# Fused set attention and feed-forward on one core: one maximum for 384 tokens, a product by slots, shared 6 KB places and a new order of the steps

## The chip, the cores and the metric

The kernel runs on one core of a Trainium2 chip. Its engines work side by side and each takes its own instructions in order: TensorE (PE; its weight loads are listed as PEld) multiplies matrices into PSUM, VectorE (DVE) and ScalarE (ACT) read PSUM and SBUF, GpSimd (POOL) works on SBUF, and SyncE (SP) issues all transfers here, which 16 DMA engines carry out. The metric is the device time of one execution in microseconds. Lines such as L535 are those of the kernel before.

## The reference

Four batches of 12480 tokens of 128 numbers go through two attention steps against 32 inducing rows, and the result through a feed-forward step with 2048 hidden units.

```python
def mab(q, kv):
    s = scale * (q @ kv.transpose(0, 2, 1))
    s = s - s.max(-1, keepdims=True)
    a = np.exp(s)
    a /= a.sum(-1, keepdims=True) + 1e-09
    return a @ kv
h = mab(I, x)                 # (B, 32, 128): the inducing rows attend to all tokens
y = mab(x, h)                 # (B, N, 128): each token attends to the 32 rows of h
# feed-forward on all 49920 rows of y:
g = y @ w_in
g = g - np.tanh(g)
out = g @ w_out
```

All numbers are float32.

## The kernel before

*The mathematics it uses.* Every row of `y` is a weighted mean of the 32 rows of `h`, so `y @ w_in` is the same mean of the 32 rows of `h @ w_in`. Around the mean of those 32 rows the function `g - tanh(g)` is taken as a straight line (its value at the mean, and its slope `tanh(mean)^2`). Then the whole feed-forward step is linear in the weights of the second attention, and there is one table `P_all[:, b, :]` of 32 x 128 numbers in a batch, so that an output row is its attention weights times that table, divided by their sum. A 129th column of ones gives the sum by the same matmul. `bound` (L587 to L649) works out at run time whether the straight line is good enough; if it is not, `general` would compute the exact form after the main part. With these inputs it is not entered.

*Tiles.* A batch is cut into 8 full tiles of 1536 tokens (`SG`) and a rest of 192. In a full tile the tokens stand in four groups `q` of 384 (`SEG`). Scores of group `q` go to partitions `32q` to `32q + 31`, one partition for each inducing row, with 384 tokens along the free dimension. `R = 3` slots `r` of 128 tokens make up the 384.

*First pass over a batch, `first` (L316 to L426).* For each tile: load `xT` (128 channels x 1536 tokens, 768 KB) on SP (L329); four matmuls against the inducing rows (L306); VectorE copies the scores to SBUF and takes the running maximum (L340). When all nine tiles are through, the maximum of the batch is turned, reduced and spread (L347 to L359). Then, for each tile: ScalarE's exponential with its sum (L394), VectorE's transpose in 32 x 32 blocks (L398), and 12 matmuls into the accumulator `hacc` (L405). The last needs the tile with tokens on partitions, in natural rows. For three tiles of four (`turned`, L313) TensorE turns `xT` by 12 transposes in three groups (L380), and ScalarE or VectorE moves each group to SBUF (L384); for every fourth tile the natural rows are loaded too, another 768 KB (L388). At the end `h` is divided by its sums and transposed (L412 to L425).

*Linear part, `linear` (L434 to L498).* `h @ w_in` (L440), a copy, two sets of turns against the matrix `centre` that subtract the mean (L448), `tanh`, the series of the value at the mean (L464 to L469), the slope part `W` (L474), then two sets of 16 matmuls against `w_out`: `down` for the slope (L483) and `base` for the value (L489). Two more small steps (L493 to L496) end in `P_all`.

*Second pass, `second` (L503 to L583).* For each tile: scores against `h` (L306 again), one transposing maximum on VectorE, per token (L515); GpSimd lays these 384 maxima on diagonals (L520), and a matmul with a matrix of ones subtracts them from the scores in PSUM (L525); ScalarE's exponential (L528); the product with `P_all` by 12 matmuls into `o_ps` (L535). `o_ps` is a single buffer of four PSUM banks; group `q` writes bank `q`, from its own 32 rows of the array. The product is planned in two halves: groups 0 and 1, then groups 2 and 3. VectorE adds and inverts the sums (L545, L546), then multiplies the first half out of PSUM (L565); the second half is copied by ScalarE (L570) and multiplied by GpSimd in SBUF (L573), or done by VectorE too. Then the tile goes out (L582).

*Weights.* `w_in` and `w_out` come as 64-bit patterns, eight chunks of 512 KB in all. Each chunk takes two ScalarE, two GpSimd and three VectorE instructions (L272 to L289) to become float32.

*What sets the order.* Nothing is ordered by hand. Each step is an `Op` with an engine (or a second choice), an assumed cost, the buffers that it reads and writes and a priority. `Plan.order` plays the steps through in time: whenever an engine is free it takes the ready step with the lowest priority number whose buffers have a free place. The sequence that comes out is then issued, engine by engine. `PLACES` says how many buffers of a kind there are: 13 `xT`, 3 `xn` (turned rows), 2 `xd` (loaded rows), 5 `ot` (output, also the weights' raw chunks), 4 PSUM banks `ps` for everything but `o_ps`. The priorities are 100 a batch, plus 5 or 10 a tile.

## Time and profile before

| what | us |
|---|---|
| median of 3 runs (lowest, highest) | 279.3 (276.66, 280.68) |
| the profiled execution | 279.22 |
| its span, first to last instruction | 277.4 |
| TensorE busy | 226.3 |
| VectorE busy | 153.7 |
| ScalarE busy | 106.2 |
| GpSimd busy | 96.1 |

The span is what the views of the profile cover; the execution is 1.8 us longer than its span. "Busy" of an engine is the time in which at least one of its instructions is shown as running; matmuls overlap each other, so that TensorE may be shown busy all the time and still have room inside. The mean granted clock of TensorE is 0.894 of full speed. DMA queue 1 moved 62.02 MB, of which 25.56 MB are the output.

In the rows of the profile, `xN` is the number of instructions; in the groups by line the numbers after the bar are the busy time, the mean nanoseconds of one, and the idle time of the engine just before them with what ended most of it. In the order of time each row has its start, its length, and in square brackets the idle time before it and what ended that. In the table by stage, each row has a stretch of the span, its length, the busy time of each engine with its instructions, the granted clock, the share of the DMA engines that was busy and GB/s.

### The profile page before, as it was taken

To read this page: it belongs to the slowest core of one execution; us is meant where nothing else is said; L and a number is where in the kernel's file an instruction comes from. 1 tells how busy PE (TensorE), PEld (TensorE's weight loads), DVE (VectorE), ACT (ScalarE), POOL (GpSimd) and SP (SyncE) were. 2 spreads that over 40 slices of the span, in tenths; PEclk is the share of its full clock that TensorE was granted. 3 is DMA by queue.
4 is the path that set the end of the run, shared out by engine and by line. 5 is a ranking of instruction groups with operands and counts; after the bars stand their busy time and mean duration, and the time that the engine had idled before them with its cause. 6 is when DMAs were issued, how large, how long until landed. Compare 5 with 4: busy or idle time off the path is not lost.

```text
span 277.4 us, 7109 instructions
## 1 busy us (share of the span) xinstructions
PE 226.3 (82%) x2926; PEld 144.5 (52%) x2926; DVE 153.7 (55%) x398; ACT 106.2 (38%) x226; POOL 96.1 (35%) x108
## 2 busy tenths in 40 slices
PE   1945029999979799999999999989998989878530
PEld 0620017756646575565666665756675566444320
DVE  2488996564555664735555676366566442444440
ACT  1353564513454642144645622267463021113310
POOL 2036751011163542135432323046344210454440
PEclk9995557999999999999999999999999795577975
DMA  6999995457197789857995868225252300243542
GB/s 228 402 420 402 318 391 200 140 166 306 28 374 281 291 302 338 309 179 248 312 343 219 309 230 326 86 113 229 116 229 116 128 4 0 113 187 156 207 178 97
DMA packets 13047, 62.54 MB, mean 225 GB/s; under 512 B 1616, under 2 KB 2768, under 8 KB 13008
## 3 DMA queue, kind: packets, MB, share of 16 engines
q1 hardware_dynamic: 13008, 62.02, 59.8%
q8 instruction: 25, 0.41, 0.6%
q14 instruction: 14, 0.11, 0.1%
HBM read 36.45 MB, written 25.56 MB: 224 GB/s over the span
## 4 chain that ended last, share of the span: by engine, by line
PE 67%; DVE 13%; DMA 6%; ACT 4%; issue 4%; SPq 1%; POOL 1%; DVEq 0%; ACTq 0%; POOLq 0%
PE o_ps L535 17%; PE ps L306 15%; PE ps L380 10%; PE ps L405 9%; PE ps L525 7%; DMA xT<-in_xT 5%; DVE ot L565 4%; ACT ot L570 3%; PE ps L448 2%; PE ps L615 2%; DMA ot<-in_w_out 2%; DVE ot L283 2%; DVE ot L282 2%; PE ps L483 1%; PE ps L440 1%
## 5 line engine op out<-in xcount | busy, mean ns | idle before, releaser
L573 POOL TENSOR_TENSOR ot<-ot,mb 128x768 f32<-128x768 f32 x32 | 47.0, 1469 | 92.7 <-ACT ot L570 92.7
L535 PE MATMUL o_ps<-P_all,ex 32*128 32x129 f32 (+1 forms) x784 | 49.3, 307 | 14.8 <-ACT ot L570 12.9
L535 PEld LDWEIGHTS o_ps<-P_all,ex 32*128 32x128 f32 (+1 forms) x784 | 41.1, 203 | 34.4 <-ACT ot L570 22.1
L520 POOL TENSOR_TENSOR dg<-fold,mb 128x384 f32<-128x384 f32 (+1 forms) x36 | 27.8, 776 | 55.6 <-DVE mb L515 49.0
L384 ACT COPY xn<-ps 128x512 f32<-128x512 f32 x50 | 28.6, 590 | 41.0 <-PE ps L380 35.9
L380 PE MATMUL ps<-ident,xT 128*128 128x128 f32 x288 | 43.0, 289 | 0.5 <-ACT xn L384 0.5
L570 ACT COPY ot<-o_ps 128x768 f32<-128x768 f32 x32 | 25.5, 798 | 38.1 <-DVE ot L565 21.0
L380 PEld LDWEIGHTS ps<-ident,xT 128*128 128x128 f32 x288 | 32.6, 146 | 12.6 <-issue 5.4
L306 PE MATMUL ps<-xT,indT_sb 128*32 128x384 f32 x256 | 29.1, 540 | 11.6 <-DMA xT<-in_xT 10.0
L545 DVE TENSOR_SCALAR S_all<-o_ps 128x12 f32<-128x12 f32 (+1 forms) x36 | 6.1, 169 | 50.8 <-PE o_ps L535 49.2
L565 DVE TENSOR_TENSOR ot<-o_ps,mb 128x768 f32<-128x768 f32 x32 | 30.4, 950 | 5.7 <-ACT ot L570 5.1
L528 ACT ACTIVATE ex<-ps 128x384 f32<-128x384 f32 (+1 forms) x36 | 16.6, 463 | 42.6 <-PE ps L525 42.6
L525 PE MATMUL ps<-dg,quad 128*128 128x384 f32 (+1 forms) x72 | 31.0, 517 | 1.6 <-POOL dg L520 1.6
L306 PE MATMUL ps<-xT,hT_all 128*32 128x384 f32 x256 | 29.3, 552 | 0.2 <-ACT xn L384 0.2
L340 DVE TENSOR_SCALAR_CACHE_REDUCE s<-ps 128x384 f32<-128x384 f32 (+1 forms) x36 | 18.3, 515 | 17.6 <-PE ps L306 17.1
L405 PE MATMUL ps<-xn,et 128*32 128x128 f32 x576 | 22.3, 288 | 6.1 <-DVE et L398 6.1
L515 DVE TRANSPOSE_TENSOR_REDUCE mb<-ps 128x12 f32<-128x384 f32 (+1 forms) x36 | 19.4, 542 | 8.9 <-PE ps L306 8.7
L405 PEld LDWEIGHTS ps<-xn,et 128*32 128x32 f32 x576 | 16.0, 114 | 12.3 <-DVE et L398 6.6
L398 DVE STREAM_TRANSPOSE et<-s 128x384 f32<-128x384 f32 (+1 forms) x36 | 18.3, 515 | 5.1 <-PE ps L405 3.6
L394 ACT ACTIVATE s<-s,nb 128x384 f32<-128x384 f32 (+1 forms) x36 | 21.1, 588 | 0.0
L384 DVE COPY xn<-ps 128x512 f32<-128x512 f32 x22 | 15.1, 688 | 7.3 <-PE ps L380 6.7
L306 PEld LDWEIGHTS ps<-xT,indT_sb 128*32 128x32 f32 x256 | 6.8, 115 | 18.9 <-issue 12.4
(110 smaller groups left out, 201.9 us busy)
## 6 DMA issues: line engine op xcount, KB each, us to landing
xT<-in_xT SPq DMA_DIRECT2D x32, 768.0 KB, 6.6
out<-ot SPq DMA_DIRECT2D x32, 768.0 KB, 3.6
xd<-in_xn SPq DMA_DIRECT2D x8, 768.0 KB, 6.0
ot<-in_w_in SPq DMA_DIRECT2D x4, 512.0 KB, 12.0
ot<-in_w_out SPq DMA_DIRECT2D x4, 512.0 KB, 5.7
xr<-in_xT SPq DMA_DIRECT2D x4, 96.0 KB, 8.8
xnr<-in_xl SPq DMA_DIRECT2D x4, 96.0 KB, 5.6
out<-otr SPq DMA_DIRECT2D x4, 96.0 KB, 3.7
```

The costliest lines, as they stand in the source:

```text
L306: nc.tensor.matmul(ps[q * m:(q + 1) * m, :sg], lhsT=w, rhs=seg(x, nq, None, q), start=True, stop=stop)
L380: nc.tensor.transpose(out=ps.get()[:, k * 128:(k + 1) * 128], in_=xt.get()[:, c:c + 128], identity=ident)
L384: copy(x.get()[:, 4 * g:4 * g + 4, :].rearrange("p k c -> p (k c)"), ps.get())
L394: nc.scalar.activation(out=t, in_=t, func=AF.Exp, scale=SC, bias=nb.get()[:P], accum_out=sums.get()[:P, s:s + 1])
L405: nc.tensor.matmul(hacc.get()[q * m:(q + 1) * m, :C], lhsT=et.get()[:P, k, :], rhs=x.get()[:P, k, :], start=(s == 0 and k < NQ), stop=last ...
L515: nc.vector.tensor_reduce(out=mb.get()[:P, :kb], in_=ps.get()[:P, :sg].rearrange("p (k i) -> p k i", i=m), axis=AX.X, op=ALU.max, apply_tr ...
L520: nc.gpsimd.tensor_tensor(out=dg.get()[:P, :kb], in0=fold[:P, 0:1, :].to_broadcast([P, kb, m]), in1=mb.get()[:P, :kb].unsqueeze(2).to_broa ...
L525: nc.tensor.matmul(ps.get()[:P, :sg], lhsT=quad2[:P, :P], rhs=dg.get()[:P, :kb].rearrange("p k i -> p (k i)"), start=False, stop=True, ski ...
L535: nc.tensor.matmul(o_ps[:T, q, r * (C + 1):(r + 1) * (C + 1)], lhsT=ex.get()[p, r * T:(r + 1) * T], rhs=P_all[p, b, :], start=True, stop=True)
L565: nc.vector.tensor_tensor(out=dst().rearrange("p (q r) c -> p q r c", r=nr), in0=o(q0, q1)[:, :, :, :C], in1=rs().rearrange("p (q r) -> p ...
L570: nc.scalar.copy(out=dst().rearrange("p (q r) c -> p q r c", r=nr), in_=o(q0, q1)[:, :, :, :C])
L573: nc.gpsimd.tensor_tensor(out=dst(), in0=dst(), in1=rs().unsqueeze(2).to_broadcast([T, w, C]), op=ALU.mult)
```

## The change

1. **Second attention.** `h` is also stored with the mean of the 32 rows taken off and the scale multiplied in (`foldx`, 32 more columns of `hT_all`). The scores are made from that. In place of one maximum per token there is one for all 384 tokens and 32 rows of a group: a plain maximum along the free dimension, then a tiny transposing one over the 32 partitions. It is the bias of the exponential. The diagonals on GpSimd and the matmul that subtracted them are gone.
2. **Last product by slots.** The product is cut by `r`: slots 0 and 1 of all four groups, then slot 2. The first piece (1024 columns) is ScalarE's first choice with GpSimd's multiplication after it, the second (512 columns) VectorE's.
3. **Places.** `xT`, natural rows (turned or loaded), outputs and raw weights share 23 places of 6 KB a partition; `MOST` allows at most 15 `xT`, 8 natural rows and 5 `ot` of them.
4. **Turned steps.** `TURNED` lists them: 7, 4, 4 and 1 tiles of the four batches, 16 in place of 24. The natural rows of the other 16 tiles are loaded, where it was 8.
5. **Linear part.** The two sets of turns become one of 132 columns into two banks; the 16 matmuls of `base` go, and GpSimd adds the value at the mean to `W` before `down`, in two halves.
6. **Weights.** One of VectorE's three instructions for a chunk becomes a step of its own (`flush`), which GpSimd may take as two instructions.
7. **Bound.** The 16 matmuls with 128 x 128 weights become 16 with 32 columns of weights, an extra copy and two gathering matmuls; the end has a few more small VectorE steps.
8. **Order.** The priorities of nearly all steps have offsets of their own (`K`), the planner adds a cost where TensorE changes the kind of matmul (`mode`), and most assumed costs are different. Batch 0's loads come before the weights' loads; the steps from the last score of a batch to `P_all` go ahead of all others (`p - 400`); the conversion of `w_out` has the priority 201.8 where it had 70.

```diff
+K = dict(load=-84.1, step1=1, copy=-159.2, step2=6.8, turn=-41.2, move=256.3, nat=-92.5, exp1=-82.5, et=-37.3, acc=-56.3,
+         sc2=-151.1, top=-102.6, exp2=-134.9, prod=-116.5, rec=-60.8, ev=-1.4, off=(-23.9, -10.7, -42.2, 91.1), step3=11.6,
+         w1=52.7, w2=201.8, bound=74.9)
+TURNED = ((0, 1, 2, 3, 4, 6, 7), (1, 2, 5, 7), (2, 3, 5, 7), (5,))
...
-    PLACES = dict(xT=13, xr=3, xn=3, xd=2, xnr=2, s1=11, et=3, ex=3, dg=2, ot=5, otr=2, mb=4, ps=4, W=1)
+    PLACES = dict(big=23, xr=3, xnr=2, s1=11, et=3, ex=3, otr=2, mb=4, ps=4, W=1)
+    MOST = dict(xT=15, xn=8, ot=5)
...
+        nc.vector.tensor_scalar(out=foldx[:, 128:], in0=foldx[:, :m], scalar1=SC, scalar2=-SC / m, op0=ALU.mult, op1=ALU.add)
...
+            def flush2(r=r):
+                nc.gpsimd.tensor_scalar(out=r["e"], in0=r["e"], scalar1=WMIN, scalar2=None, op0=ALU.is_ge)
+                nc.gpsimd.tensor_tensor(out=r["v"], in0=r["e"], in1=r["v"], op=ALU.mult)
...
-            add("DVE", 2.1, bits, reads=[], writes=[buf, outs[k]], pri=p)
+            add("DVE", 0.7, flush, writes=[buf], pri=p, POOL=(1.9, flush2))
+            add("DVE", 1.4, bits, reads=[], writes=[buf, outs[k]], pri=p)
...
-                writes=[x], pri=pri + s - 30, lag=2)
+                writes=[x], pri=pri + s + K["load"], lag=2)
...
-        add("PE", 0.6, down, reads=[W, *wout_b], writes=[psP], pri=pri)
-        add("PE", 0.6, base, reads=[lin_b[b], *wout_b], writes=[psP], pri=pri)
+        def raised(k):
+            nc.gpsimd.tensor_tensor(out=part(W.get(), k), in0=part(W.get(), k), in1=part(g, k).unsqueeze(2).to_broadcast([128, NF // 2, m]), op=ALU.add)
...
+        add("PE", 0.9, down, reads=[W, *tan_parts, *wout_b], writes=[psP], pri=pri, mode="c")
...
         def top():
-            nc.vector.tensor_reduce(out=mb.get()[:P, :kb], in_=ps.get()[:P, :sg].rearrange("p (k i) -> p k i", i=m), axis=AX.X,
-                                    op=ALU.max, apply_transpose=True, negate=True)
...
-        def lower():
-            nc.tensor.matmul(ps.get()[:P, :sg], lhsT=quad2[:P, :P], rhs=dg.get()[:P, :kb].rearrange("p k i -> p (k i)"),
-                             start=False, stop=True, skip_group_check=True)
...
+            nc.vector.tensor_reduce(out=mb.get()[:P, 0:1], in_=ps.get()[:P, :sg], axis=AX.X, op=ALU.max)
+            nc.vector.tensor_reduce(out=mb.get()[:P, 1:2], in_=mb.get()[:P, 0:1].to_broadcast([P, m]), axis=AX.X, op=ALU.max,
+                                    apply_transpose=True, negate=True)
...
+        cuts = ((0, 2), (2, 3)) if full else ((0, 1),)
+
+        def product(r0, r1):
+            for r in range(r0, r1):
+                for q in range(nq):
                     p = slice(q * m, (q + 1) * m)
                     nc.tensor.matmul(o_ps[:T, q, r * (C + 1):(r + 1) * (C + 1)], lhsT=ex.get()[p, r * T:(r + 1) * T],
                                      rhs=P_all[p, b, :], start=True, stop=True)
...
+            ways = dict(DVE=(0.15 + 0.135 * w, whole), ACT=(0.19 + 0.1 * w, plain))
+            one_way = ("ACT", "DVE")[k]
+            done = add(one_way, *ways.pop(one_way), reads=[mb, o_b[k], ot], writes=[part], pri=pri + K["ev"], **ways)
+            add("POOL", 0.1 + 0.235 * w, norm, reads=[mb, ot], writes=[part], pri=pri,
+                needed=lambda done=done: done.eng == "ACT")
...
-    weight(w_in, win_sb, win_b, 60, -26.5)
-    weight(w_out, wout_sb.rearrange("p f d -> p (f d)"), wout_b, 70, -22.5)
+    weight(w_in, win_sb, win_b, K["w1"], -21.5)
+    weight(w_out, wout_sb.rearrange("p f d -> p (f d)"), wout_b, K["w2"], -17.5)
     for b in range(B):
         first(b, 100.0 * b)
         for s in range(NSG):
-            second(b, s, 100.0 * (b + 1) + 10 * s)
-    bound(100.0 * B - 20)
+            second(b, s, 100.0 * (b + 1) + K["off"][b] + K["step3"] * s)
+    bound(100.0 * B + K["bound"])
```

More of the change, by code (lines that the diff above doesn't have):

```diff
@@ L450, in linear @@
[L450 to L459 removed]
+        mean, g = mean_all[:, b, :], g_all[:, b, :]
@@ L461, in series @@
+        for k in range(2):
+            add("PE", 0.46, lambda k=k: turn(k), reads=[Y, centre_b], writes=[psM[k]], pri=pri, mode="f")
+            add("DVE", 0.17, lambda k=k: nc.vector.tensor_copy(part(mean, k).rearrange("p (t j) -> p t j", j=NQ), view(k)[:, :, 128:]),
+                reads=[psM[k]], writes=[mean_parts[k]], pri=pri)
+        add("ACT", 0.25, lambda: nc.scalar.activation(out=th.get(), in_=mean, func=AF.Tanh),
+            reads=mean_parts, writes=[th], pri=pri)
         def series():
@@ L514, in top @@
         def top():
-            nc.vector.tensor_reduce(out=mb.get()[:P, :kb], in_=ps.get()[:P, :sg].rearrange("p (k i) -> p k i", i=m), axis=AX.X,
-                                    op=ALU.max, apply_transpose=True, negate=True)
-        add("DVE", 0.53 if full else 0.25, top, reads=[ps], writes=[mb], pri=pri)
-        def diagonal():
-            nc.gpsimd.tensor_tensor(out=dg.get()[:P, :kb], in0=fold[:P, 0:1, :].to_broadcast([P, kb, m]),
-                                    in1=mb.get()[:P, :kb].unsqueeze(2).to_broadcast([P, kb, m]), op=ALU.mult)
@@ L522, in second @@
-        add("POOL", 0.85 if full else 0.35, diagonal, reads=[mb, fold_b], writes=[dg], pri=pri)
-        def lower():
-            nc.tensor.matmul(ps.get()[:P, :sg], lhsT=quad2[:P, :P], rhs=dg.get()[:P, :kb].rearrange("p k i -> p (k i)"),
-                             start=False, stop=True, skip_group_check=True)
-        add("PE", 0.4, lower, reads=[dg, quad_b], writes=[ps], pri=pri)
-        add("ACT", 0.51 if full else 0.3, lambda: nc.scalar.activation(out=ex.get()[:P, :sg], in_=ps.get()[:P, :sg], func=AF.Exp, scale=SC),
-            reads=[ps], writes=[ex], pri=pri)
@@ L531, in product @@
-        def product(q0, q1):
-            for r in range(nr):
-                for q in range(q0, q1):
+            nc.vector.tensor_reduce(out=mb.get()[:P, 0:1], in_=ps.get()[:P, :sg], axis=AX.X, op=ALU.max)
+            nc.vector.tensor_reduce(out=mb.get()[:P, 1:2], in_=mb.get()[:P, 0:1].to_broadcast([P, m]), axis=AX.X, op=ALU.max,
+                                    apply_transpose=True, negate=True)
+        add("DVE", 0.7 if full else 0.4, top, reads=[ps], writes=[mb], pri=pri + K["top"])
@@ L534, in product @@
+        add("ACT", 0.55 if full else 0.3, lambda: nc.scalar.activation(
+            out=ex.get()[:P, :sg], in_=ps.get()[:P, :sg], func=AF.Exp, bias=mb.get()[:P, 1:2]), reads=[ps, mb], writes=[ex], pri=pri + K["exp2"])
+        cuts = ((0, 2), (2, 3)) if full else ((0, 1),)
+        def product(r0, r1):
+            for r in range(r0, r1):
+                for q in range(nq):
                     p = slice(q * m, (q + 1) * m)
@@ L536, in product @@
                                      rhs=P_all[p, b, :], start=True, stop=True)
-        for h in range(2):
-            add("PE", 0.37 if full else 0.25, lambda h=h: product(h * nq // 2, (h + 1) * nq // 2), reads=[ex, P_b[b]], writes=[o_b[h]], pri=pri)
-        def o(q0, q1):
-            return o_ps[:T, q0:q1, :nr * (C + 1)].rearrange("p q (r c) -> p q r c", c=C + 1)
+        for k, (r0, r1) in enumerate(cuts):
+            add("PE", (0.22 * (r1 - r0) + 0.03) if full else 0.25, lambda r0=r0, r1=r1: product(r0, r1), reads=[ex, P_b[b]], writes=[o_b[k]],
+                pri=pri + K["prod"], mode="r")
@@ L608, in terms @@
             v.scalar_tensor_tensor(out=c[:, 1], in0=g_all, scalar=-1.0, in1=g_all, op0=ALU.mult, op1=ALU.max)
-        add("DVE", 1.3, terms, reads=[*lin_b], writes=[cols, absm, r, *dev_b], pri=pri)
-        def pe():
-            for n, (t, j) in enumerate((t, j) for t in range(4) for j in range(4)):
-                f = 4 * j + t
-                w = (wabs, wabs2)[f // half].get()[:, f % half, :]
-                nc.tensor.matmul(ps.get()[:, :2 * B], lhsT=w, rhs=cols.get()[:, 4 * t + j, :], start=(n == 0), stop=(n == NF - 1))
@@ L616, in bound, with sums @@
-        add("PE", 2.5, pe, reads=[wabs, wabs2, cols], writes=[ps], pri=pri)
+        add("DVE", 1.6, terms, reads=[*lin_b], writes=[cols, absm, r2, *dev_b], pri=pri)
+        def sums():
+            for t in range(4):
+                for j in range(4):
+                    f = 4 * j + t
+                    nc.tensor.matmul(ps.get()[j * m:(j + 1) * m, :C], lhsT=cols.get()[:, 4 * t + j, :],
+                                     rhs=(wabs, wabs2)[f // half].get()[:, f % half, :], start=(t == 0), stop=(t == 3))
@@ L618, in least, with gather @@
+        add("PE", 0.95, sums, reads=[wabs, wabs2, cols], writes=[ps], pri=pri, mode="c")
+        add("ACT", 0.3, lambda: nc.scalar.copy(out=G.get(), in_=ps.get()[:, :C]), reads=[ps], writes=[G], pri=pri)
+        def gather():
+            for k in range(2):
+                nc.tensor.matmul(ps2.get()[:B, k * C:(k + 1) * C], lhsT=fold2[:, k:2 * B:2], rhs=G.get(), start=True, stop=True)
+        add("PE", 0.5, gather, reads=[G, fold_b], writes=[ps2], pri=pri, mode="x")
         def least():
             v = nc.vector
-            c = ps.get()[:, :2 * B].rearrange("p (b k) -> p k b", k=2)
```

272 lines of the change are left out of this document (146 added, 126 removed).

## The prediction

> **What bounds the kernel now.** I read the page first (busy times, chain, DMA queues), then the busy time by stage, the groups by line and shape, and last the order of time at the three places where the stage changes.
>
> ```profile
> span 277.4 us, 7109 instructions
> PE 226.3 (82%) x2926; PEld 144.5 (52%) x2926; DVE 153.7 (55%) x398; ACT 106.2 (38%) x226; POOL 96.1 (35%) x108
> ...
> q1 hardware_dynamic: 13008, 62.02, 59.8%
> ...
> PE 67%; DVE 13%; DMA 6%; ACT 4%; issue 4%; SPq 1%; POOL 1%; DVEq 0%; ACTq 0%; POOLq 0%
> PE o_ps L535 17%; PE ps L306 15%; PE ps L380 10%; PE ps L405 9%; PE ps L525 7%; DMA xT<-in_xT 5%; DVE ot L565 4%; ACT ot L570 3%; PE ps L448 2%; PE ps L615 2%; DMA ot<-in_w_out 2%; DVE ot L283 2%; DVE ot L282 2%; PE ps L483 1%; PE ps L440 1%
> ```
>
> The chain is two thirds TensorE, and its largest lines are the last product (L535), the scores, the turns (L380) and the diagonal matmul (L525). But the mean hides stages:
>
> ```profile
> core 0: us, PE busy (x) PEld busy (x) DVE busy (x) ACT busy (x) POOL busy (x), PEclk, DMA share, GB/s
> 0.00:20.00 20.00, 11.28 (x84) 6.20 (x84) 9.36 (x27) 7.73 (x12) 4.27 (x23) 1.00 0.90 348
> 20.00:44.80 24.80, 9.22 (x90) 4.54 (x91) 22.85 (x35) 10.71 (x23) 15.96 (x14) 0.52 0.98 375
> 44.80:71.60 26.80, 26.53 (x391) 17.54 (x389) 14.72 (x43) 11.17 (x24) 2.45 (x3) 1.00 0.46 163
> 71.60:227.30 155.70, 147.41 (x2086) 96.02 (x2082) 89.82 (x247) 67.55 (x152) 57.08 (x54) 0.99 0.62 228
> 227.30:267.40 40.10, 30.44 (x277) 19.69 (x276) 14.77 (x37) 8.77 (x15) 14.52 (x13) 0.74 0.33 134
> 267.40:277.40 10.00, 1.42 (x6) 0.56 (x6) 2.21 (x11) 0.28 (x2) 1.82 (x2) 0.50 0.31 111
> ```
>
> To 44.8 the DMA engines are full (0.90, 0.98) and VectorE, which converts the weights, nearly so (22.85 of 24.80); TensorE waits. From 44.8 to 227.3 TensorE is the bound: 173.9 busy of 182.5, DMA at 0.46 and 0.62. From 227.3 (batch 3's `P_all` complete) no engine is full: a chain through the one `o_ps` buffer. Then 10 us of end.
>
> ```profile
> 71.64 1.28 PE L535 MATMUL o_ps<-P_all,ex 32*128 32x129 f32 x24
> ...
> 227.06 0.27 ACT L496 COPY P_all<-ps 128x128 f32<-128x128 f32 x1 [0.58 <-PE ps L494]
> ...
> 259.75 1.28 PE L535 MATMUL o_ps<-P_all,ex 32*128 32x129 f32 x24 [1.41 <-ACT ot L570]
> ...
> 261.15 0.17 DVE L545 TENSOR_SCALAR S_all<-o_ps 128x12 f32<-128x12 f32 x1 [2.14 <-PE o_ps L535]
> ...
> 261.69 0.96 DVE L565 TENSOR_TENSOR ot<-o_ps,mb 128x768 f32<-128x768 f32 x1
> ...
> 262.72 0.80 ACT L570 COPY ot<-o_ps 128x768 f32<-128x768 f32 x1 [0.26 <-DVE ot L565]
> ...
> 263.57 1.28 PE L535 MATMUL o_ps<-P_all,ex 32*128 32x129 f32 x24 [1.39 <-ACT ot L570]
> ```
>
> One tile takes 263.57 - 259.75 = 3.82 us: product, sums, VectorE's half, ScalarE's half, next product, each behind the other, although the halves lie in different banks.
>
> **The change, part by part.**
>
> ```profile
> L535 PE MATMUL o_ps<-P_all,ex 32*128 32x129 f32 (+1 forms) x784 | 49.3, 307 | 14.8 <-ACT ot L570 12.9
> L525 PE MATMUL ps<-dg,quad 128*128 128x384 f32 (+1 forms) x72 | 31.0, 517 | 1.6 <-POOL dg L520 1.6
> L520 POOL TENSOR_TENSOR dg<-fold,mb 128x384 f32<-128x384 f32 (+1 forms) x36 | 27.8, 776 | 55.6 <-DVE mb L515 49.0
> L380 PE MATMUL ps<-ident,xT 128*128 128x128 f32 x288 | 43.0, 289 | 0.5 <-ACT xn L384 0.5
> L384 ACT COPY xn<-ps 128x512 f32<-128x512 f32 x50 | 28.6, 590 | 41.0 <-PE ps L380 35.9
> L570 ACT COPY ot<-o_ps 128x768 f32<-128x768 f32 x32 | 25.5, 798 | 38.1 <-DVE ot L565 21.0
> L565 DVE TENSOR_TENSOR ot<-o_ps,mb 128x768 f32<-128x768 f32 x32 | 30.4, 950 | 5.7 <-ACT ot L570 5.1
> L573 POOL TENSOR_TENSOR ot<-ot,mb 128x768 f32<-128x768 f32 x32 | 47.0, 1469 | 92.7 <-ACT ot L570 92.7
> ...
> L615 PE MATMUL ps<-cols,ot 128*128 128x8 f32 x32 | 4.8, 290 | 0.0
> L489 PE MATMUL ps<-wout_sb,g_all 128*32 128x128 f32 x128 | 4.3, 273 | 0.0
> L573 POOL TENSOR_TENSOR otr<-otr,mb 96x128 f32<-96x128 f32 x4 | 1.6, 396 | 1.3 <-ACT otr L570 1.2
> L565 DVE TENSOR_TENSOR otr<-o_ps,mb 96x128 f32<-96x128 f32 x4 | 1.1, 279 | 0.0
> L570 ACT COPY otr<-o_ps 96x128 f32<-96x128 f32 x4 | 1.0, 261 | 6.1 <-DVE S_all L545 4.7 <-DVE otr L565 1.4
> ```
>
> *Diagonal matmul.* 31.0 us of TensorE and 27.8 of GpSimd go. A second, tiny VectorE reduction per tile comes: nothing to 0.28 us (the 96x128 row), I take 0.2, 7 us in all, and the exponential gets a bias. Both lie in VectorE's and ScalarE's idle time (89.82 and 67.55 of 155.7 busy) and ahead of the product; without that cover 7 us would be paid.
>
> *Product by slots.* Before, two row groups run abreast and the second half catches up with the first: alone, a half takes
>
> ```profile
> 194.63 0.94 PE L535 MATMUL o_ps<-P_all,ex 32*128 32x129 f32 x12
> ```
>
> against 1.28 for both. By slots, four row groups run abreast, in the six steps of one half. Bounds 0.94 and 1.28; I take 0.94, as the second half's 0.34 shows that four do overlap. 32 tiles x 0.94 = 30.1, so 19.2 of 49.3 us go (some of it half-clock time). The pieces become two thirds and one third: ScalarE 1024 columns by (798 - 261)/640 = 0.84 ns a column, 1.01; VectorE 512 by 1.05 ns, 0.68; together 1.69 where 1.75 was. Both read all four banks, so they stay one behind the other, as they are now. GpSimd's pass over the larger piece grows to 1.90, 61 us for 47.0, less than the 27.8 it loses. The tile's chain: 3.82 - 0.34 - 0.06 = 3.42.
>
> *Turned steps, 24 to 16.* 96 transposes at 43.0/288 us: 14.3 of TensorE; 24 copies at 0.59: 14 us of ScalarE and VectorE, hidden now and then. In their place 8 loads of 768 KB (6.29 MB).
>
> *Second linear step and bound.* L489's 4.3 us go; eight GpSimd additions come (half the W tile each, under 0.78, the mean of the `dg` row), 1 to 1.5 us in each batch's chain, covered by other tiles' work until batch 3. L615's 32 matmuls become 32 like L489's, 4.3/4 = 1.1: 3.7 saved, at the tail's head. The end has two more short VectorE steps: 0.4.
>
> *Places and order.* `xT` gets up to 15 places, natural rows 8 instead of 5; batch 0's loads pass ahead of all weight loads on SP's queue, and the maximum's chain ahead of VectorE's weight work. Now that chain waits in VectorE's queue:
>
> ```profile
> 29.55 0.16 DVE L347 TENSOR_REDUCE mx<-mxg 128x1 f32<-128x9 f32 x1
> ...
> 36.34 0.14 DVE L359 TENSOR_SCALAR nb<-ps 128x1 f32<-128x1 f32 x1
> ```
>
> Some 4 of these 6.8 us go, the loads come some 6 us sooner, and with 7 turned tiles of batch 0 allowed places early its first product should start near 50 instead of 71.6. What is moved back is `w_out`'s conversion: four loads, eight ScalarE, eight or more GpSimd and twelve VectorE instructions; if it is late, batch 0's `P_all` is.
>
> **The sum.** TensorE's whole work becomes 226.3 - 31.0 - 19.2 - 14.3 - 4.3 - 3.7 = 153.8. To 44.8 some 20.5 of it lies as now, in tail and end about 15.7 (eight products and scores at half to 0.9 us each, and the end's 1.4): 117.6 between. The DMA work is 0.598 x 277.4 = 165.9 us for 62.02 MB (374 GB/s); 6.29 MB more make 182.7. To 44.8 the engines do 0.90 x 20 + 0.98 x 24.8 = 42.3 as now, in tail and end 0.33 x 40.1 + 0.31 x 10 = 16.3. So 124.1 us of DMA stand against 117.6 of TensorE: DMA takes the bound over, closely. How full it gets lies between 0.90 and full:
>
> ```profile
> 10.00:20.00 10.00, 7.18 (x65) 3.55 (x64) 6.42 (x17) 5.86 (x10) 2.33 (x3) 1.00 1.01 407
> ...
> 100.00:110.00 10.00, 10.00 (x171) 6.26 (x164) 4.71 (x14) 3.08 (x6) 3.81 (x4) 1.00 0.90 320
> ```
>
> I take 0.95: 130.6, so batch 3's `P_all` at 175.4. Tail 8 x 3.42 = 27.4, end 10.4: span 213.2. The profiled execution took 279.2 with a span of 277.4 (the median of three runs is 279.3), so 1.8 more: 215.
>
> **The clock in the tail.** There TensorE will be busy about 1.8 of 3.42 us a tile.
>
> ```profile
> 231.60:236.90 5.30, 3.68 (x33) 2.15 (x32) 2.85 (x11) 0.80 (x1) 0.79 (x1) 0.50 0.00 0
> ...
> 259.70:263.50 3.80, 2.42 (x28) 1.57 (x28) 1.36 (x3) 1.27 (x3) 1.77 (x2) 1.00 0.52 210
> ```
>
> Busier (3.68 of 5.30), it was at half clock; less busy (2.42 of 3.80), at full. I take full, since what stood ahead of the cold stretch, the 128x8 matmuls, goes; at half clock the product's 0.94 doubles at most and the tail is up to 7.5 longer. The Trainium skill (TensorE: Matmul & The Clock Gate, The HAM clock gate) has the clock fall after an idle window of about 3.4 us: by it the sum stays at 215. The first row does not agree: half clock without such a gap; by that row the sum is up to 222.
>
> **The rivals.**
> 1. *DMA is not the bound.* At the 407 GB/s of 10 to 20 us the 124.1 become 114, TensorE's 117.6 decides: 44.8 + 117.6 + 27.4 + 10.4 + 1.8 = 202; less where batch 0's turns move ahead of 44.8. For it: that row. Against: reads alone ran so; with writes among them the best row has 320 at 0.90. The Trainium skill (Perfetto Trace Analysis, Roofline) gives the 16 DMA engines about 435 GB/s together; by it the DMA work is an estimated 157 us and this rival holds. No window quoted here reaches it. 0.17.
> 2. *Loads stand behind outputs.* SP issues in order, and waits for finished outputs:
>
> ```profile
> SPq L582 <- POOL ot L573: 82.0, 30, 14.4
> ```
>
> GpSimd's longer pass makes each output later. At a DMA share of 0.75 the 124.1 take 165: 250. 0.20.
> 3. *`w_out` late.* Batch 0's first product at 71.6 as now. All 23 places are then full after about 59 us of transfers (23 at 2.1 and weights), and of 182.7 - 59 - 16.3 = 107 are left at 71.6: 184 + 27.4 + 10.4 + 1.8 = 224. The change to the start then gives nothing. 0.10.
> 4. *Slower.* As rival 2, in full: the share stays at the present 0.62, 200 us for 124.1, 285 in all. It decides below 0.64. Against: TensorE kept it at 0.62, since loads waited for places. 0.04; about no change 0.03.
>
> **How the numbers follow.** Forecast 0.46 (205 to 232, the cold tail in it): 215. The range 200 to 246 leaves out the lower part of rival 1, the upper of 2, and 4. A measurement tells about 2% from no change: faster 0.93, within 0.03, slower 0.04.
>
> **What would show it.** Right: no L525; the product near 0.94; the first product near 50; DMA above 0.9 and TensorE under 0.9 busy from 45 to 175; tail tiles 3.4 us apart. Wrong: a DMA share near 0.75 with TensorE waiting for `xT`, products at 1.28, or tail tiles above 4 us.

## The result and the profile after

| | before | after |
|---|---|---|
| median (lowest, highest), us | 279.16 (276.66 to 280.68), 4 runs | 225.57 (222.63 to 229.22), 4 runs |
| ratio, 95% interval | 1 | 0.8023 [0.7901, 0.8145] |
| profiled execution, its span | 279.2, 277.4 | 224.91, 223.3 |
| mean granted clock of TensorE | 0.894 | 0.897 |

The ratio leaves out the two slower runs of the changed kernel, 226.23 and 229.22.

The page of the changed kernel:

```profile
span 223.3 us, 6466 instructions
PE 167.2 (75%) x2603; PEld 103.8 (46%) x2603; DVE 143.7 (64%) x437; ACT 105.0 (47%) x205; POOL 104.0 (47%) x91
...
q1 hardware_dynamic: 14160, 68.31, 79.9%
...
PE 31%; DVE 19%; DMA 19%; ACT 12%; POOL 10%; issue 6%; SPq 1%; ACTq 0%; DVEq 0%; POOLq 0%
```

TensorE's share of the chain falls from 67% to 31%, that of DMA transfers rises from 6% to 19%, and no engine has a majority any more. The table by stage, cut at the changed kernel's own first product (66.2), the last batch's `P_all` (180.9) and the last product (212.2):

```profile
20.00:44.80 24.80, 18.90 (x314) 13.51 (x311) 21.20 (x50) 15.42 (x35) 18.53 (x16) 0.86 0.98 368
44.80:66.20 21.40, 16.54 (x214) 9.95 (x203) 17.58 (x46) 13.06 (x32) 15.62 (x13) 1.00 0.80 309
66.20:180.90 114.70, 96.59 (x1702) 59.70 (x1702) 78.88 (x263) 58.35 (x113) 51.66 (x33) 0.97 0.90 341
180.90:212.20 31.30, 19.96 (x283) 12.02 (x276) 14.78 (x42) 11.87 (x16) 14.33 (x8) 0.66 0.47 190
212.20:223.30 11.10, 1.10 (x7) 0.28 (x5) 2.23 (x12) 0.37 (x1) 1.48 (x2) 0.50 0.24 87
```

The columns are those of the prediction's table. The middle took 155.7 us before and takes 114.7 now; the start is 5.4 shorter, the tail 8.8, the end 1.1 longer: 54.1 in all. In the middle the DMA engines are at 0.90 and TensorE at 96.59/114.70 = 0.84, so on this table alone the DMA engines look like the bound, as predicted. The experiments say otherwise.

The single instructions cost what was expected of them, except where the clock is low (the mean of the product's matmuls is 321 ns against 307 before, though the product as a whole takes less time at full clock, that is, warm):

```profile
L572 PE MATMUL o_ps<-P_all,ex 32*128 32x129 f32 (+1 forms) x784 | 39.1, 321 | 23.4 <-DVE big L605 16.3
```

One tile in the middle at full clock, in order of time:

```profile
126.81 0.95 PE L572 MATMUL o_ps<-P_all,ex 32*128 32x129 f32 x24 [0.63 <-ACT big L608]
...
127.90 0.17 DVE L586 TENSOR_SCALAR S_all<-o_ps 128x12 f32<-128x12 f32 x1 [0.85 <-PE o_ps L572]
128.10 1.01 ACT L608 COPY big<-o_ps 128x1024 f32<-128x1024 f32 x1 [0.36 <-DVE S_all L586]
...
129.15 0.69 DVE L605 TENSOR_TENSOR big<-o_ps,mb 128x512 f32<-128x512 f32 x1 [0.75 <-ACT big L608]
129.89 0.95 PE L572 MATMUL o_ps<-P_all,ex 32*128 32x129 f32 x24 [0.54 <-DVE big L605]
```

and one in the tail:

```profile
200.63 1.67 PE L572 MATMUL o_ps<-P_all,ex 32*128 32x129 f32 x24 [0.62 <-DVE big L605]
...
202.37 0.17 DVE L586 TENSOR_SCALAR S_all<-o_ps 128x12 f32<-128x12 f32 x1 [1.09 <-PE o_ps L572]
...
204.36 1.67 PE L572 MATMUL o_ps<-P_all,ex 32*128 32x129 f32 x24 [1.59 <-DVE big L605]
```

It is the same chain twice: product, sums, ScalarE's piece, VectorE's piece, next product. From product to product it takes 129.89 - 126.81 = 3.08 us warm and 204.36 - 200.63 = 3.73 in the tail. From the sums to the next product it is 1.99 us both times; only the product's own part grew, from 1.09 to 1.74 before the sums start. In the waits between 66.2 and 180.9, that chain is what TensorE's matmuls mostly stand for (total, times, longest):

```profile
PE o_ps L572 <- DVE big L605: 8.0, 11, 2.3
...
PE ps L341 <- DMA big<-in_xT: 4.9, 3, 2.2
PE o_ps L572 <- ACT big L608: 3.8, 6, 1.2
```

Of the 114.70 - 96.59 = 18.1 us without a matmul, 8.0 + 3.8 = 11.8 lie before a product that waits for `o_ps` to be read out, and 4.9 before first scores whose tile hasn't landed.

### The profile page after: what moved, and what is told of

Same layout as the page of the kernel before. It is cut to its first block, busy times and chain, and to the rows that moved or that the text cites. A ratio compares the mean times of both kernels' runs of the same rounds, so it can differ in the third digit from the quotient of the medians.

```text
span 223.3 us, 6466 instructions
## 1 busy us (share of the span) xinstructions
PE 167.2 (75%) x2603; PEld 103.8 (46%) x2603; DVE 143.7 (64%) x437; ACT 105.0 (47%) x205; POOL 104.0 (47%) x91
## 3 DMA queue, kind: packets, MB, share of 16 engines
q1 hardware_dynamic: 14160, 68.31, 79.9%
## 4 chain that ended last, share of the span: by engine, by line
PE 31%; DVE 19%; DMA 19%; ACT 12%; POOL 10%; issue 6%; SPq 1%; ACTq 0%; DVEq 0%; POOLq 0%
ACT big L608 10%; PE o_ps L572 10%; DMA big<-in_xT 10%; PE ps L341 9%; DVE big L605 7%; DMA out<-big 5%; PE ps L415 5%; DMA big<-in_xn 3%; PE ps L440 3%; POOL big L309 2%; POOL win_sb L323 2%; PE ps L532 2%; POOL big L611 2%; POOL big L300 2%; DVE mb L559 2%
## 5 line engine op out<-in xcount | busy, mean ns | idle before, releaser
L611 POOL TENSOR_TENSOR big<-big,mb 128x1024 f32<-128x1024 f32 (+1 forms) x34 | 62.9, 1851 | 80.0 <-ACT big L608 78.6
L572 PE MATMUL o_ps<-P_all,ex 32*128 32x129 f32 (+1 forms) x784 | 39.1, 321 | 23.4 <-DVE big L605 16.3
L608 ACT COPY big<-o_ps 128x1024 f32<-128x1024 f32 (+1 forms) x34 | 33.3, 986 | 20.2 <-DVE S_all L586 12.2
L563 ACT ACTIVATE ex<-ps,mb 128x384 f32<-128x384 f32 (+1 forms) x36 | 19.9, 553 | 41.2 <-DVE mb L560 22.0
L341 PE MATMUL ps<-big,indT_sb 128*32 128x384 f32 x256 | 27.9, 514 | 12.9 <-DMA big<-in_xT 11.2
L440 PE MATMUL ps<-big,et 128*32 128x128 f32 x768 | 29.7, 293 | 4.7 <-DVE et L433 4.7
L605 DVE TENSOR_TENSOR big<-o_ps,mb 128x512 f32<-128x512 f32 x30 | 20.6, 688 | 18.9 <-ACT big L608 18.0
L341 PE MATMUL ps<-big,hT_all 128*32 128x384 f32 x256 | 29.9, 525 | 0.0
L415 PE MATMUL ps<-ident,big 128*128 128x128 f32 x192 | 28.1, 289 | 0.0
L440 PEld LDWEIGHTS ps<-big,et 128*32 128x32 f32 x768 | 22.6, 118 | 10.2 <-DVE et L433 5.6
L415 PEld LDWEIGHTS ps<-ident,big 128*128 128x128 f32 x192 | 21.7, 146 | 9.7 <-issue 5.4
L375 DVE TENSOR_SCALAR_CACHE_REDUCE s<-ps 128x384 f32<-128x384 f32 (+1 forms) x36 | 18.2, 514 | 11.8 <-PE ps L341 11.6
L419 DVE COPY big<-ps 128x512 f32<-128x512 f32 x20 | 13.5, 678 | 4.0 <-PE ps L415 3.9
```

Source lines behind the costliest of these rows:

```text
L341: nc.tensor.matmul(ps[q * m:(q + 1) * m, :sg], lhsT=w, rhs=seg(x, nq, None, q), start=True, stop=stop)
L415: nc.tensor.transpose(out=ps.get()[:, k * 128:(k + 1) * 128], in_=xt.get()[:, c:c + 128], identity=ident)
L419: copy(x.get()[:, 4 * g:4 * g + 4, :].rearrange("p k c -> p (k c)"), ps.get())
L440: nc.tensor.matmul(hacc.get()[q * m:(q + 1) * m, :C], lhsT=et.get()[:P, k, :], rhs=x.get()[:P, k, :], start=(s == 0 and k < NQ), stop=last ...
L563: add("ACT", 0.55 if full else 0.3, lambda: nc.scalar.activation(out=ex.get()[:P, :sg], in_=ps.get()[:P, :sg], func=AF.Exp, bias=mb.get()[ ...
L572: nc.tensor.matmul(o_ps[:T, q, r * (C + 1):(r + 1) * (C + 1)], lhsT=ex.get()[p, r * T:(r + 1) * T], rhs=P_all[p, b, :], start=True, stop=True)
```

## The experiments

The question was what sets the middle: the DMA engines (the prediction), TensorE with its queue, or the chain through `o_ps`. Beside it stood the late start and the tail. Each run below is the changed kernel with one edit, except where before is named. The kernel before was run beside each, on the same chip, so that what is compared are the ratios to it; a difference of two ratios is given in us by way of 279.2. The changed kernel's own interval, 0.790 to 0.8145, is 3.4 us to either side: smaller differences from it are not told apart. Stages are read from one profiled execution each. Where an edit adds a step or alters a cost or a priority, the order of the steps is planned anew, so more than the edited step can move.

**More work for TensorE.** One matmul of 128 x 128 by 384 columns ahead of the second scores of each of the 32 full tiles; the scores overwrite its result.

```diff
+        def both():
+            if full:
+                nc.tensor.matmul(ps.get()[:, :sg], lhsT=quad2, rhs=x.get()[:, :sg], start=True, stop=True)
+            scores(ps.get(), x.get(), nq, sg, hT_all[:, b, 128:], True)
```

> The changed kernel with one more matmul in each of the 32 full tiles of the second pass: 128x128 weights against 384 columns, the size of the removed diagonal matmul, written to the same PSUM bank just ahead of the scores that overwrite it. Nothing else is added, no wait on GpSimd. It costs TensorE 32 x 0.65 to 0.9 = 21 to 29 us. Theory (DMA bounds the middle, TensorE was busy 96.6 of 114.7 us there): most of the idle time takes it up, 230 to 238 us. Rival (TensorE still bounds): the whole of it is paid, 247 to 254. Rival (the chain through o_ps bounds every stage): under 230.

Measured: 237.25 us, ratio 0.8552 [0.8472, 0.8632], (0.8552 - 0.8023) x 279.2 = 14.8 more than the changed kernel. By the total this is the DMA theory's number. The stage table of this run says that the total came about in another way:

```profile
65.20:198.90 133.70, 116.39 (x1814) 64.32 (x1810) 81.62 (x265) 60.38 (x121) 49.87 (x31) 1.00 0.80 294
198.90:225.40 26.50, 17.29 (x253) 9.45 (x251) 14.14 (x40) 10.85 (x15) 14.35 (x8) 0.92 0.52 209
```

The middle became 133.7 - 114.7 = 19.0 us longer, for 116.4 - 96.6 = 19.8 us more of TensorE's busy time, and the DMA share fell from 0.90 to 0.80. If the DMA engines had set the middle, the 18.1 us in which TensorE wasn't busy would have swallowed most of it. The tail became 4.8 us shorter, with more work in it:

```profile
206.11 0.95 PE L576 MATMUL o_ps<-P_all,ex 32*128 32x129 f32 x24 [0.48 <-DVE big L609]
...
209.15 0.95 PE L576 MATMUL o_ps<-P_all,ex 32*128 32x129 f32 x24 [0.46 <-DVE big L609]
```

Tiles 209.15 - 206.11 = 3.04 apart where the changed kernel has 3.73: this tail ran at full clock until its last products. That isn't shown to be the added matmul's doing: the new plan also put `bound`'s 32 matmuls ahead of batch 3's `P_all` (at 197.12), and the run with before's priorities, below, has such a tail without any matmul added.

**Fewer bytes.** Only half of each loaded natural tile is loaded, and the accumulation reads that half twice; the other half of these rows is left out of the computation. TensorE issues as many matmuls as before.

```diff
-                    out=x.get(), in_=xn[LOADED.index((b, s))] if s < NS else xl[b]), ...
+                    out=x.get()[:, :KB // 2] if s < NS else x.get(), in_=xn[LOADED.index((b, s))][:, :KB // 2] if s < NS else xl[b]), ...
...
+                    j = k if s == NS or turned(b, s) else k % (KB // 2)
```

> The changed kernel with each of the 16 loads of natural rows cut to half its bytes (6 of 12 blocks; the accumulation uses those six twice, so half of these rows is left out of the computation). Plan, order and every engine's work are as in the changed kernel; only 6.3 MB of transfers, 16.8 us of all DMA engines, are gone. Theory (DMA sets the middle, with the o_ps chain close behind it at 3.0 to 3.7 us a tile): 6 to 14 us shorter, 211 to 219. Rival (the o_ps chain and TensorE's queue set it, DMA is busy but not waited for): 221 to 228.

Measured: 223.12 us (222.43 to 225.48), ratio 0.8108 [0.7958, 0.8259]: no gain over the changed kernel's 0.8023. With 6.3 MB of 68.3 gone, the middle of the profiled execution is

```profile
69.40:178.70 109.30, 93.17 (x1702) 57.29 (x1702) 78.10 (x259) 57.37 (x109) 51.67 (x33) 1.00 0.83 308
```

5.4 us shorter, 3.4 of it in TensorE's busy time (clock 1.00 in place of 0.97) and 2.0 in its waits, and it begins 3.2 us later. The waits for `xT` at the head of TensorE's queue fall from 4.9 to 2.9 us, and between 69.4 and 178.2 the clock is never at half, as it was from 112.3 to 115.7 in the changed kernel. So the loads do cost the middle a few us. But the DMA share drops to 0.83, and of the theory's 6 to 14 us nothing shows in the whole (by the medians alone it would be 2.5): the rival's reading.

**Every natural tile loaded twice.**

```diff
+                    for _ in range(2 if s < NS else 1):
+                        nc.sync.dma_start(out=x.get(), in_=xn[LOADED.index((b, s))] if s < NS else xl[b])
```

> The changed kernel with each of the 16 loads of natural rows issued twice into the same place: 12.6 MB more, 33.6 us of all DMA engines at 374 GB/s, nothing more for any other engine. Theory (DMA bounds the middle): 22 to 33 us longer, 246 to 258. Rival (TensorE or the o_ps chain bounds, DMA is only busy): under 235, as 20 per cent of the DMA time was idle.

Measured: 302.54 us, ratio 1.0906 [1.0801, 1.101], some 45 us above what either theory allowed. The experiment tested something else. On SP's queue:

```profile
SPq L425 <- DMA big<-in_xn: 127.8, 16, 12.0
```

The second load writes the place that the first writes, so SP waits for the first to land, 16 times and 127.8 us in all, and every load and output behind it on the queue waits too. It says nothing of the DMA engines' capacity, and shows what a wait on that queue costs.

**The product by row groups again, one `o_ps`.** Two halves of two groups each; VectorE and ScalarE take 768 columns each, as before.

```diff
-        cuts = ((0, 2), (2, 3)) if full else ((0, 1),)
+        cuts = ((0, nq // 2), (nq // 2, nq))
...
-            for r in range(r0, r1):
-                for q in range(nq):
+            for r in range(nr):
+                for q in range(q0, q1):
```

> The changed kernel with the last product cut by groups again, as before the change (two halves of two groups each, one o_ps buffer), ScalarE's and VectorE's pieces 768 columns each; all else as changed, planned anew. TensorE pays 0.34 us a tile more where the halves run together and 0.94 where they do not, 11 to 30 us in all, and the chain through o_ps grows from some 3.05 to 3.4 us a tile at full clock. Theory now (the chain through o_ps and TensorE's queue in front of it set the middle, since half of the natural rows' transfers was worth only 2 us): 233 to 245. Rival (DMA sets the middle): 224 to 230.

Measured: 244.12 us, ratio 0.8725 [0.8626, 0.8823]: beside the rest of the change, the slots are worth (0.8725 - 0.8023) x 279.2 = 19.6 us. The middle:

```profile
68.30:195.40 127.10, 108.31 (x1722) 71.90 (x1718) 84.71 (x254) 55.80 (x119) 41.30 (x34) 0.94 0.79 303
```

12.4 longer for 11.7 more of TensorE's time: one for one again, and the time is in the range of the theory, 233 to 245.

**The same with two buffers.** `o_ps` as two tiles of two banks, each half its own.

```diff
-    o_ps = ps_o.tile([128, NQ, 512], F32, name="o_ps")
+    o_two = [ps_o.tile([128, 2, 512], F32, name=f"o_ps{h}") for h in range(2)]
...
-    o_b = [fixed(o_ps), fixed(o_ps)]
+    o_b = [fixed(o_two[0]), fixed(o_two[1])]
```

> As the halves by groups, but o_ps is two buffers of two banks each in place of one of four, so that nothing orders ScalarE's piece, VectorE's piece and the next product's other half; one more short VectorE sum per tile. Theory (the chain through o_ps sets middle and tail): from some 3.4 us a tile the chain comes down to 2.2 to 2.9, which more than pays for TensorE's 0.34 to 0.94: 210 to 221. Rival (TensorE's own time is what counts, the chain is hidden): as the halves with one buffer or longer, 230 to 245. Rival (DMA sets it): 222 to 228.

Measured: 232.2 us, ratio 0.8347 [0.8278, 0.8415]: 10.6 less than with one buffer, so the chain through the single buffer does cost, but 9.0 more than the changed kernel. That is in the range of the rival by which TensorE's own time counts; the 210 to 221 of the theory, that the chain through `o_ps` sets middle and tail, were not reached.

```profile
65.70:189.90 124.20, 109.27 (x1722) 73.27 (x1718) 87.17 (x281) 55.38 (x120) 41.32 (x34) 0.90 0.82 313
```

In the middle the time without a matmul falls to 14.9 us, and hardly any of it is for `o_ps` any more; most of it now lies before scores whose tile hasn't landed:

```profile
PE ps L341 <- DMA big<-in_xT: 9.1, 2, 4.7
...
PE o_ps L572 <- ACT big L610: 1.6, 1, 1.6
```

Most of the gain lies outside the middle (the first product starts 2.6 earlier, the middle is 2.9 shorter, the rest is behind it). Slots with two buffers would need eight banks; that wasn't tried.

**Before, with the one maximum alone.** The centred `h`, one maximum and the bias; no diagonal matmul. All else as before.

> The kernel before with the first part of the change alone: centred h, one maximum for 384 tokens, bias in the exponential, no diagonals on GpSimd and no diagonal matmul; order, halves, places and turned tiles as before. TensorE loses 31.0 us, of which 22.0 in the middle stage that it bounds. Theory: 250 to 258 us. Rival (the longer VectorE step, 0.55 and 0.21, takes the place of the GpSimd step in the chain and gives the gain back): 265 or more.

Measured: 274.17 us, ratio 0.9868 [0.9772, 0.9964]: (1 - 0.9868) x 279.2 = 3.7 us where the 31.0 us matmul went: the rival's number, not the 250 to 258 of the theory. The middle of this kernel:

```profile
71.60:221.40 149.80, 132.86 (x2030) 89.51 (x2029) 96.18 (x276) 68.74 (x149) 36.44 (x27) 0.94 0.64 236
```

TensorE's busy time fell by 14.6 (the clock fell too, to 0.94), and the time without a matmul rose from 8.3 to 16.9. The matmul went out of a queue that then stood waiting instead. Its waits before the product are 17.2 us for ScalarE and 7.8 for VectorE over the span, in the rows below, where the first was 12.9 before; in the middle alone the two make 10.0 where they made 5.0. There ScalarE's exponential waits 29.2 us for VectorE's maximum; it waited 23.0 for the diagonal matmul. That fits the rival, by which the longer VectorE step takes the place of the step that went.

```profile
PE o_ps L528 <- ACT ot L563: 17.2, 10, 2.6
...
PE o_ps L528 <- DVE ot L558: 7.8, 8, 1.8
```

**The changed kernel with the priorities of before.** `K`, the `p - 400` steps and the weights' priorities set back to before's.

```diff
-K = dict(load=-84.1, step1=1, copy=-159.2, step2=6.8, turn=-41.2, move=256.3, nat=-92.5, ...
+K = dict(load=-30, step1=5, copy=0, step2=5, turn=-10, move=-10, nat=-40, ...
...
-            reads=[mxg, *mx_parts], writes=[mx], pri=p - 400)
+            reads=[mxg, *mx_parts], writes=[mx], pri=p)
```

> The changed kernel with the priorities of the kernel before (5 a tile, 10 a tile, no step ahead of others, weights at 60 and 70, loads of batch 0 mixed with the weights), all computations, places, turned tiles and assumed costs as after. Theory: the DMA engines are kept less full without the new order, a share near 0.75 in the middle, 235 to 250 us. Rival (the order is most of the gain): 260 or more. Rival (the order gives nothing beside the removed work): 219 to 232.

Measured: 236.3 us, ratio 0.8492 [0.841, 0.8573]. The time is in the theory's range and the DMA share near its 0.75. The order is worth (0.8492 - 0.8023) x 279.2 = 13.1 us, and little of it at the start: the first product is at 67.62 here. Middle and tail of its profiled execution, which is 2.4 us above its median:

```profile
67.60:201.30 133.70, 105.95 (x1818) 66.47 (x1814) 85.85 (x277) 62.25 (x127) 50.37 (x32) 0.94 0.79 294
201.30:227.40 26.10, 14.25 (x240) 8.63 (x241) 12.46 (x36) 10.84 (x15) 14.35 (x8) 0.83 0.53 212
```

Here TensorE is without a matmul for 27.7 us, 9.6 more than in the new order, and at a lower clock. The middle is 19.0 us longer; the tail, with nothing of `bound` left in it (its matmuls start at 194.78 here), is 5.2 shorter than the changed kernel's, at full clock from 204.7 to 221.7 though no work was added:

```profile
211.19 0.95 PE L571 MATMUL o_ps<-P_all,ex 32*128 32x129 f32 x24 [1.32 <-DVE big L604]
...
214.22 0.95 PE L571 MATMUL o_ps<-P_all,ex 32*128 32x129 f32 x24 [1.30 <-DVE big L604]
```

**24 turned tiles.**

```diff
-TURNED = ((0, 1, 2, 3, 4, 6, 7), (1, 2, 5, 7), (2, 3, 5, 7), (5,))
+TURNED = ((0, 1, 2, 4, 5, 6),) * 4
```

> The changed kernel with 24 turned steps, as before, in place of 40: about 6.3 MB more to load (what the fewer turned steps had taken off again put differently: the steps' forms as before), and TensorE loses or gains the turns of 16 steps, 12 to 14 us, with as much on ScalarE and VectorE for the copies. Theory now (the chain through the one o_ps buffer and TensorE's queue in front of it set the middle): what matters is the work added to TensorE and the copying engines, 228 to 238 us. Rival (the DMA engines set the middle, as predicted): fewer bytes, 210 to 221 us.

The expectation's first sentence misstates the edit: 24 turned tiles stand in place of 16, not of 40; 6.3 MB less are loaded and eight tiles more are turned, which is what its two ranges are for. Measured: 241.6 us, ratio 0.8616 [0.8557, 0.8674], 16.6 more than the changed kernel with 6.3 MB less: far from the DMA theory's 210 to 221, and some 4 above the other's range. But it isn't a clean test of either, since the edit spoilt the start. SP's own queue, in order of time:

```profile
62.92 12.16 SPq L364 DMA_DIRECT2D big<-in_xT  x2
```

and its waits:

```profile
SPq L364 <- POOL wout_sb L323: 18.1, 3, 11.4
```

Two loads of `xT` take SP 12.16 us to issue, up to 11.4 of them waiting for a place that a raw chunk of `w_out` holds until GpSimd has joined it: the price of sharing the places. The first product starts at 79.64, 13.5 later than in the changed kernel.

**The start: `w_out` sooner; GpSimd without the flush.** Two edits.

```diff
-         w1=52.7, w2=201.8, bound=74.9)
+         w1=52.7, w2=56.7, bound=74.9)
```

> The changed kernel with the priority of w_out's conversion at 56.7 in place of 201.8, right behind w_in's; all else the same (the plan is drawn up anew). Theory (batch 0's table waited for w_out's last chunk at 61.3 to 62.6 us, and the first product for the table): the table of batch 0 4 to 9 us earlier, the whole 3 to 9 us shorter, 216 to 222. Rival (what is won at the start is given back in the middle, which the DMA engines set): 223 to 229.

```diff
-            add("DVE", 0.7, flush, writes=[buf], pri=p, POOL=(1.9, flush2))
+            add("DVE", 0.7, flush, writes=[buf], pri=p)
```

> The changed kernel without GpSimd as a second choice for the flush of the weights: five chunks took 1.61 and 1.31 us of GpSimd there, 14.6 us between 25 and 62 us in which GpSimd was 8.8 to 9.8 of 10 busy; VectorE takes them in 1.07 each, 5.4 us. Theory (GpSimd is what makes w_out late): the table of batch 0 4 to 9 us earlier, 216 to 222. Rival (VectorE, 8 to 9.5 of 10 busy there, becomes as late): 223 to 230.

Measured: 225.29 us, ratio 0.8155 [0.8077, 0.8233], and 225.22 us (221.07 to 228.53), ratio 0.8162 [0.7915, 0.841]. Both are the rivals' numbers, and neither differs from the changed kernel's ratio by more than the intervals allow. The first product started at 67.78 and at 64.17, where it was 66.17. Taking 17 us of work from GpSimd moved it by 2.

**The tail: TensorE kept busy.** Two matmuls of 512 columns behind each product of batch 3.

```diff
+            def keep():
+                for j in range(2):
+                    nc.tensor.matmul(psd.get(), lhsT=ident, rhs=win_sb[:, j * 512:(j + 1) * 512], start=True, stop=True)
```

> The changed kernel with two more matmuls of 128x128 weights against 512 columns behind each product of batch 3 (0.87 us of TensorE a full tile at full clock), whose result nobody reads. Theory (the clock falls in the tail because TensorE is busy for about half of the time, and the half clock makes the product 1.68 in place of 0.94): the clock stays full, a tile takes about 3.05 where it took 3.73, 4 to 6 us shorter, 218 to 221. Rival (the half clock is no matter in the tail, or the added matmuls only delay the next product): 225 or more.

Measured: 226.08 us, ratio 0.8162 [0.8016, 0.8307]: the rival's number, with the theory's clock. In the tail of its profiled execution, which is 3.0 us above the median:

```profile
197.37 0.95 PE L572 MATMUL o_ps<-P_all,ex 32*128 32x129 f32 x24
198.25 1.98 PE L583 MATMUL ps<-win_sb,ident 128*128 128x512 f32 x4
```

The product is warm at 0.95, but the added pair takes 1.98 us (each is issued as two), so that TensorE is full (29.6 of the tail's 30.5 us) and gives back what the clock gave.

**Both together, with the smaller matmul.** No flush on GpSimd, and the 384-column matmul of the first experiment in batch 3's tiles alone.

```diff
-            add("DVE", 0.7, flush, writes=[buf], pri=p, POOL=(1.9, flush2))
+            add("DVE", 0.7, flush, writes=[buf], pri=p)
...
+            if full and b == B - 1:
+                nc.tensor.matmul(ps.get()[:, :sg], lhsT=quad2, rhs=x.get()[:, :sg], start=True, stop=True)
```

> The changed kernel without GpSimd's part in the flush of the small weights, and with one extra 128x128x384 matmul ahead of the scores in the full tiles of batch 3 alone, meant to keep TensorE's granted clock up. Theory: the tail goes from 31.3 us to about 25 (8 tiles 3.05 apart), so 215 to 220 us. Rival: the clock falls all the same, or the added matmuls take what the clock gives: 223 to 229 us.

Measured: 222.04 us (221.42 to 224.92, 6 runs), ratio 0.795 [0.7911, 0.7989]: between the two ranges. That is 2.0 us below the changed kernel, and the interval lies within that one's [0.7901, 0.8145], so a gain is not shown. In the profiled execution, the slowest of the six, half clock came back in the tail twice all the same, for 3.4 us from 193.8 on, behind a product that had waited 2.11 us for ScalarE, and from 207.4 to its end.

## Why the prediction was right, and where it wasn't

The stretch from the first product to batch 3's `P_all`, over the runs that bear on it (TensorE's rest is the length less its busy time):

| kernel | length | TensorE busy | rest | DMA share |
|---|---|---|---|---|
| before | 155.7 | 147.4 | 8.3 | 0.62 |
| after | 114.7 | 96.6 | 18.1 | 0.90 |
| half the natural bytes | 109.3 | 93.2 | 16.1 | 0.83 |
| one matmul more a tile | 133.7 | 116.4 | 17.3 | 0.80 |
| product by groups | 127.1 | 108.3 | 18.8 | 0.79 |
| by groups, two buffers | 124.2 | 109.3 | 14.9 | 0.82 |
| before's priorities | 133.7 | 106.0 | 27.7 | 0.79 |

In the five rows from after to the two buffers, the length goes with TensorE's busy time and the rest stays at 15 to 19; with before's priorities the rest grows. The DMA share has no such part. The middle is set by TensorE's one queue: its work, plus a rest. In the changed kernel the larger part of the rest is the product at the head of the queue, waiting for `o_ps` (11.8 of 18.1); by groups it is shared with tiles that haven't landed (7.0 of 18.8), and with two buffers the tiles are most of it (9.1 of 14.9). So the loads come close behind `o_ps`. Followed back, the chain that ended last in the changed kernel's middle also runs through transfers for 32% of its length (loads of `xT` 15.0%, outputs 10.5%, natural rows 6.5%). That the rest as a whole could be removed, no run shows.

- **The step that failed: "DMA takes the bound over, closely".** It compared 124.1 us of DMA work with 117.6 of TensorE work and gave TensorE's waits nothing. TensorE was busy 16.5 + 96.6 = 113.1 us from 44.8 to 180.9, near the 117.6; beside that it stood for 4.9 us before the first product and 18.1 behind it. 113.1 + 23.0 = 136.1, where the sum had 130.6 from the DMA share. That the sum came within 6 us there, and the whole within 5%, is luck: two different things were of about the same size. Its sign, DMA above 0.9 and TensorE under 0.9, was nearly met (0.90 and 0.84), and didn't tell the two apart: 6.3 MB could go from under the share of 0.90 for no measured gain.
- **The parts.** The product by slots was taken at 0.94 and takes 0.95; ScalarE's piece 1.01 and 1.01; VectorE's 0.68 and 0.69; GpSimd's 1.90 and 1.90. The bytes are the predicted 62.02 + 6.29 = 68.31 MB. The DMA work is 0.799 x 223.3 = 178.4, predicted 182.7.
- **TensorE's whole work**: 167.2 for 153.8. Of the 13.4, 39.1 - 30.1 = 9.0 lie in the product: 2.3 are the four rests, which the 30.1 left out, and five tiles of the tail ran at 1.67 for 0.95, 3.6 in all. That the part from 44.8 on came out near is again two errors against each other: TensorE did 33.0 us of its work before 44.8, where the sum had 20.5 "as now".
- **The first product**, "near 50", came at 66.2. The loads and batch 0's first pass were early, as said; `w_out` wasn't. What the third rival has as its mechanism is the one that occurred, at a smaller size. The end of the conversion, in order of time:

```profile
61.33 1.29 POOL L323 TENSOR_TENSOR wout_sb<-wout_sb,big 128x512 uint32<-128x512 uint32 x1 [0.63 <-DVE nb L394]
...
62.67 0.95 PE L532 MATMUL ps<-wout_sb,W 128*32 128x128 f32 x25 [1.51 <-POOL wout_sb L323]
```

  The linear step's last 25 matmuls start 0.05 us after the last chunk is joined. The two runs meant to bring it forward didn't; that `w_out` is late is shown, what it would take to have it sooner, and whether that pays, is open.
- **The tail**, 27.4, took 31.3. The errors have opposite signs. The chain of a tile was put at 3.42 and is 3.08 warm: the 0.34 are what lay between the sums and the first piece before (261.15 to 261.69, 0.54, the reciprocal among it) less what lies there now (127.90 to 128.10, 0.20), since the piece that goes first is now ScalarE's plain copy, which needs no reciprocal. Against that stand the clock and a wait. The clock was taken full; it was granted at 0.66 on average over the tail, at half up to 184.0 and again from 194.2 on. At 3.73 a tile, half clock costs 0.65 each. The wait is in the tile whose product starts at 188.85; the next one starts 4.77 us later. Four small steps of `bound` on VectorE (188.71 to 190.57) and the next tile's maximum stand ahead of its sums:

```profile
188.71 0.27 DVE L668 TENSOR_SCALAR bt_t<-ps 4x128 f32<-4x128 f32 x1
...
191.21 0.13 DVE L586 TENSOR_SCALAR S_all<-o_ps 128x12 f32<-128x12 f32 x1
```

  The clock falls right behind that wait. The prediction named half clock and priced it at up to 7.5. The run with before's priorities, with no such wait, had tiles 3.03 apart and a tail of 26.1, so the two together are worth some 5 us. In the two runs for the start the same wait, 2.96 us, stood in the tail, but the clock held behind it, to 200.7 and further; these tails took 28.9 and 29.0, so some 2.4 of the 5 are the clock's. And the wait alone doesn't make the clock fall.
- **The Trainium skill** (TensorE: Matmul & The Clock Gate, The HAM clock gate) has the clock fall after an idle window of about 3.4 us. The prediction set it beside its full clock, whose ground was that the 128x8 matmuls go. The tail had no idle time that long and was at half clock all the same: the row from before that disagreed was the one to follow. Its longest, 3.04 us:

```profile
193.62 0.62 PE L572 MATMUL o_ps<-P_all,ex 32*128 32x129 f32 x12 [3.04 <-ACT big L608]
```

  The same page's section on a second failure mode has the clock swing between its two states where TensorE is idle for short times around cycled PSUM banks. The trace agrees in part: the short idle times are here, but from 194.2 to its end the tail stayed at half.
- **The rivals.** Rival 1 was right that the DMA engines aren't the bound and wrong on its 202, for want of the 23 us of waits and of the tail's clock and wait. Rivals 2 and 4 did not occur: the DMA share stayed at 0.90.
- **The whole.** `P_all` of batch 3 came 5.5 later than forecast (180.9 for 175.4), tail 3.9, end 0.7: together 10.1. The profiled execution took 223.3 + 1.6 = 224.91 where 213.2 + 1.8 = 215 was forecast.

## What to carry to other kernels

A busy share near 0.9 names a candidate for the bound, not the bound: take some of its work away and add some to its neighbour, and read the stage's length against each. In a sum by stage, an engine that works in order through a single buffer needs a term for its waits beside its work; here 11.8 us in 115, and 4.9 more for tiles that hadn't landed. In a chain of short steps, look at which consumer goes first: the one that needs the fewest results of its sister engine takes a whole step off the chain.
